# Two sections of small-tile work per chunk on TensorE, and new planning dates, in a fused linear recurrence and SwiGLU kernel

## The chip, the cores and the metric

The kernel runs on one core of a Trainium2 chip, in fp32. The metric is the time of one execution on the device in microseconds. TensorE multiplies matrices, VectorE (DVE) and ScalarE (ACT) work on elements, GpSimd (POOL) does a few small things, and SyncE (SP) issues most of the transfers. PSUM has eight banks, into which TensorE writes.

## The reference

```python
# attention block: batch 4, 8 heads, 768 steps, head size 48
scale = np.minimum(mag, 0.999) / (mag + 1e-06)          # mag = |a_re + i a_im|
a_re_n, a_im_n = (a_re * scale, a_im * scale)
for t in range(S):
    new_re = ar * S_re - ai * S_im                      # ar, ai: the gates of step t, per row d
    new_im = ar * S_im + ai * S_re
    kv = np.einsum('bhd,bhe->bhde', k[:, :, t], v[:, :, t])
    S_re, S_im = (new_re + kv, new_im)
    y[:, :, t] = np.einsum('bhd,bhde->bhe', q[:, :, t], S_re)
# then, on x = y as 3072 tokens of 384
rms = np.sqrt(np.mean(x * x, axis=-1, keepdims=True) + 1e-06)
xn = x / rms * rms_g
g = xn @ w_gate                                         # 384 x 1536
silu = g * (1.0 / (1.0 + np.exp(-g)))
val = xn @ w_val                                        # 384 x 1536
return (silu * val @ w_out).astype(np.float32)          # 1536 x 384
```

## The kernel before, in words

The sequence is cut into 24 chunks of 128 steps (six for each batch). The gates' cumulated products turn q and k into 96 rows per head (two parts of 48), so that a chunk's recurrence becomes matrix products. `attend(n)` does a chunk:

- **Scores.** k times q, four heads (one half) in a bank, in small tiles of 96 x 32. VectorE copies each half under a causal mask into `am` (COPY_PREDICATED).
- **y.** `am` times v (tiles `ve`), and q times the state of the chunk before, both in small tiles, into bank 6.
- **State.** k is transposed by TensorE with `ident` in full tiles, ScalarE copies the two halves into `kt`, and `kt` times v (tile `vn`) in small tiles makes the chunk's share of the state in bank 5. VectorE adds the old state and multiplies by the decay.
- **Norm.** ScalarE squares y into `sq`, VectorE adds its three parts, `ones` times `sq` on TensorE sums over the features into one column of bank 7. VectorE scales it into `ssv`, GpSimd raises it to the power -0.5 (`rs`), two transfers on the POOL queue spread it over the partitions (`sq<-rs`, `row<-sq`), and VectorE multiplies y by `row` into `xT`.

From the fifth chunk on (`n >= LATER`, 4) both halves of the scores use bank 5, one after the other, and both halves of the transposed k use bank 7. A work item of TensorE in small tiles carries `mode=BLK`; y and state are two items, which the planner may place apart.

Two chunks make a group of the feed-forward part. The first two groups use plain products (`feed`); the other ten use a bilinear scheme with fewer products (`joint`, with sums of `xT` in the tiles `yg` and `ve2`, of the weights in `in`, `rot`, `kq`, `am`), whose partial results go round the banks 0 to 4 by copies on ScalarE and sums on VectorE. The products with w_out (`wo`, `sums`, with `hT`) follow for each group.

Nothing is issued where it is written. Every operation is recorded by `add` with an estimated duration, what it reads and writes, and a date by which it is due; `schedule` then plays the engines forward in time and picks on each free engine the ready operation with the earliest date. That order is issued (all operations carry the line of `issue`, so tiles tell them apart). `shift` moves the dates of a stage of a chunk (such as ("norm", 16)) by so many microseconds. `between` adds a price where TensorE changes its tile, `grip` marks VectorE operations among SBUF tiles, `shy` GpSimd operations that are planned to wait for these.

The small tiles and full tiles meet in this planner like this:

```python
        if o["mode"] is not None:
            return 0.09
        return 0.13 if last["stage"][0] == "attend" else 0.01
```

Of the kernel before, what the change touches and what calls it, by code (L numbers as in the profile page):

```python
# [14 lines left out]
ALU = mybir.AluOpType  # L15
# [4 lines left out]
C = 128  # L20
BLK = 32
CAP = 0.999
EPS_MAG = 1e-6
EPS_RMS = 1e-6
# [476 lines left out]
class Flow:  # L501
# [9 lines left out]
    LANES = 8  # L511
    turn = 0.0
    patient = ("ACT", "DVE")
# [21 lines left out]

    def between(self, o, last):
# [41 lines left out]

    def add(self, eng, calls, dur, reads=(), writes=(), table=None, land=None, due=None, after=(), behind=(), late=None, mode=None, group=None):
# [4 lines left out]
        op = dict(i=len(self.ops), eng=eng, calls=calls, dur=dur, deps=set(), table=table, land=land, over=over, grip=grip, shy=shy,  # L584
                  base=due, late=late, mode=mode, group=group, stage=self.stage, behind={o["i"] for o in behind})
# [30 lines left out]
    def schedule(self):  # L616
        users = self.dates()
        left = [len(op["deps"]) + len(op["behind"]) for op in self.ops]
        ready = [0.0] * len(self.ops)
        free = {}  # L620
        waiting = {}
        table = None
        mode = last = None
        for op in self.ops:
            free.setdefault(op["eng"], self.BEGIN.get(op["eng"], 0.0))
            waiting.setdefault(op["eng"], [])
# [5 lines left out]
        served = held = 0.0  # L632
        order = 0

        def release(o, end, users=users):
            for u in users[o["i"]]:
                x = self.ops[u]
                ready[u] = max(ready[u], end + self.delay(o, x))
                left[u] -= 1
                if not left[u]:  # L640
                    waiting[x["eng"]].append(x)

        while True:
            best = None
            for eng, ops in waiting.items():
                if ops:
                    t = max(free[eng], min(ready[o["i"]] for o in ops))
                    if eng == "POOL":
                        t = min(max(free[eng], ready[o["i"]], held + 0.01 if o["shy"] else 0.0) for o in ops)
                    if eng == "SP" and len(sent) >= self.LANES:  # L650
# [18 lines left out]
            for o in waiting[eng]:  # L669
                if ready[o["i"]] > t + 1e-9 or o["shy"] and t < held:  # L670
                    continue
                key = o["due"]
                if o["table"] and table not in self.TABLES[o["table"]]:
                    key += self.switch
                if eng == "PE" and o["mode"] != mode:
                    key += self.turn
                if pick is None or key < pick[0]:
                    pick = (key, o)
            o = pick[1]
            if eng in self.patient:  # L680
                for x in waiting[eng]:
                    if t < ready[x["i"]] < t + o["dur"] - 0.2 and x["due"] < o["due"] - 50.0 and ready[x["i"]] < t + 1.5:
                        pick = None
                        free[eng] = max(free[eng], min(ready[y["i"]] for y in waiting[eng] if t < ready[y["i"]]))
                        break
                if pick is None:
                    continue
# [8 lines left out]
            if o["grip"]:  # L696
                held = t + dur
            if eng == "PE":
                dur += self.between(o, last)
                mode, last = o["mode"], o  # L700
# [6 lines left out]
            if eng == "PE":  # L707
                busy = sum(min(e, t) - max(b, t - 4.0) for b, e in recent if e > t - 4.0)
# [25 lines left out]
def fast(tc, ctx, qT, kT, v, a_re, a_im, w_gate, w_val, w_out, rms_g, out, H, bad):  # L734
# [48 lines left out]
    flow = Flow(nc, rooms)  # L783
    flow.switch = 4.0
    add = flow.add
# [94 lines left out]
    def mm_time(n, m=P):  # L880
        return 2 * max(0.844e-3 * n, 0.872e-3 * m)
# [346 lines left out]
    def attend(n):  # L1228
# [46 lines left out]
        order = [lines[c][i] for i in range(len(lines[0])) for c in range(4)]  # L1275
        mms(order, len(order) * mm_time(C) / 4 * 1.06, mode=BLK)
        flow.stage = "state", n
        if not last:
            kt = kts[0]
            for a in range(2):  # L1280
                ps = banks[7 - 3 * a] if n < LATER else banks[7]
                kp = ps[:, 0:HH * D2].rearrange("t (h d) -> t h d", h=HH)
                calls = [(nc.tensor.transpose, (kp[:, h], k[:, a * HH + h], ident[0:D2, 0:D2]), {})
                         for h in range(HH)]
                add("PE", calls, HH * 0.095, [k[:, a * HH:(a + 1) * HH], ident], [kp])
                act(kt[:, a * HH:(a + 1) * HH], kp, AF.Copy)
            ps = banks[5][0:D2, 0:DM]
            st = ps.rearrange("p (h d) -> p h d", h=H)
            mms([(st[c * BLK:(c + 1) * BLK, h], kt[:, h, c * BLK:(c + 1) * BLK], vv[:, h], True, True)
                 for h in range(H) for c in range(3)], H * 0.1, mode=BLK)  # L1290
            st4 = ps.rearrange("p (m e d) -> p m e d", m=NP, e=2)
# [338 lines left out]
    for in_, limit, op in ((ef, P_MIN, ALU.is_ge), (ef, 1.0, ALU.is_le), (range_, 0.0, ALU.is_le),  # L1630
# [17 lines left out]
    flow.shift = {  # L1648
        ("attend", 1): 2.0, ("attend", 2): -2.1, ("attend", 3): 16.0, ("attend", 4): 0.2, ("attend", 7): 4.7,
        ("attend", 14): -3.2, ("attend", 18): 6.6, ("decay", 1): 4.4, ("feed", 0): 15.4, ("feed", 1): 12.3,  # L1650
        ("feed", 2): 2.4, ("feed", 3): 0.1, ("feed", 4): 3.5, ("feed", 5): 22.0, ("feed", 6): 4.5,
        ("feed", 7): 47.1, ("feed", 8): -19.0, ("feed", 9): 11.6, ("feed", 10): 2.4, ("feed", 11): -11.1,
        ("form", 7): -0.2, ("form", 13): 6.0, ("load", 2): -16.5, ("load", 11): -2.1, ("look", 0): 9.4,
        ("look", 10): -10.6, ("norm", 16): -36.5, ("norm", 17): 36.0, ("norm", 22): -0.4, ("raw", 1): 19.8,
        ("root", 3): 2.8, ("root", 9): 0.2, ("root", 11): -9.6, ("rot", 3): -0.3, ("rot", 10): 58.8,
        ("scale", 0): 9.5, ("size", 0): 11.7, ("size", 3): 59.8, ("size", 8): -27.7, ("size", 10): 10.7,
        ("size", 11): -5.5, ("state", 0): 3.8, ("state", 3): -0.4, ("state", 4): -4.8, ("state", 6): -9.3,
        ("state", 7): -15.4, ("state", 10): -1.9, ("state", 13): -10.7, ("state", 16): 5.4, ("state", 18): 20.1,
        ("state", 21): -10.5, ("state", 22): 0.6, ("turn", 0): -1.4, ("turn", 1): 3.3, ("turn", 3): -0.4,
# [3 lines left out]
    }  # L1663
# [53 lines left out]
```

## Time and profile before

| | |
|---|---|
| three runs | 702.35, 703.12, 703.64 us; median 703.12 |
| span of the profiled execution | 699.7 us, from its first to its last instruction |
| TensorE busy | 648.4 us (93%) |
| weight loads of TensorE (beside its products) | 601.9 us (86%) |
| VectorE busy | 560.1 us (80%) |
| ScalarE busy | 506.9 us (72%), of that 67 table loads with 86.0 us |
| GpSimd busy | 71.5 us (10%) |
| mean granted TensorE clock | 0.995 |

A run's time is some 3 us above the span, since it holds what lies before the first and after the last instruction. In rows of the timeline stand the start in us from the beginning of the span, the duration, the engine, line and operation, the tile that is written and what it is made from, the TensorE tile (such as 96\*32), shapes and a count; in brackets the idle time before it and what ended it. An fp32 product shows as two MATMULs in the trace and as one row in an order of the program. A line of waits gives the total in us, how often, and the longest.

### The profile page before, as it was taken

To read this page: it belongs to the slowest core of one execution; us is meant where nothing else is said; L and a number is where in the kernel's file an instruction comes from. 1 tells how busy PE (TensorE), PEld (TensorE's weight loads), DVE (VectorE), ACT (ScalarE), POOL (GpSimd) and SP (SyncE) were. 2 spreads that over 40 slices of the span, in tenths; PEclk is the share of its full clock that TensorE was granted. 3 is DMA by queue.
4 is the path that set the end of the run, shared out by engine and by line. 5 is a ranking of instruction groups with operands and counts; after the bars stand their busy time and mean duration, and the time that the engine had idled before them with its cause. 6 is when DMAs were issued, how large, how long until landed. Compare 5 with 4: busy or idle time off the path is not lost.

```text
span 699.7 us, 18979 instructions
## 1 busy us (share of the span) xinstructions
PE 648.4 (93%) x7890; PEld 601.9 (86%) x7893; DVE 560.1 (80%) x1049; ACT 506.9 (72%) x850; POOL 71.5 (10%) x108
## 2 busy tenths in 40 slices
PE   0679999999997999999999999999999999899996
PEld 0569876886997989999999999989999989799996
DVE  7999999889987779879988969789789866255562
ACT  8677886993863974857787687685789676799860
POOL 3231030100013001001111001011000100000000
PEclk9999999999999999999999999999999999999999
DMA  9896575542334154254645205544422455744400
GB/s 293 266 282 152 148 229 147 128 81 73 90 56 81 35 116 75 70 119 87 160 89 104 69 5 115 141 84 75 118 70 55 110 118 142 244 138 155 139 1 29
DMA packets 104015, 82.02 MB, mean 117 GB/s; under 512 B 41936, under 2 KB 94416, under 8 KB 103920
## 3 DMA queue, kind: packets, MB, share of 16 engines
q1 hardware_dynamic: 98560, 64.78, 34.7%
q0 software_dynamic: 4416, 15.35, 10.2%
q8 instruction: 64, 1.05, 0.6%
q10 hardware_dynamic: 944, 0.59, 0.3%
q14 instruction: 31, 0.25, 0.1%
HBM read 55.84 MB, written 4.72 MB: 87 GB/s over the span
## 4 chain that ended last, share of the span: by engine, by line
PE 42%; issue 16%; DMA 14%; ACT 13%; DVE 10%; SPq 2%; POOL 2%; DVEq 0%; POOLq 0%; ACTq 0%
PE bank L731 42%; DMA wo<-in_w_gate_dram 3%; DMA in<-in_a_im_dram 2%; SPq L731 2%; ACT rot L731 2%; DVE hT L731 2%; ACT L731 2%; ACT hT L731 2%; ACT bank L731 1%; DMA sq<-rs 1%; DMA rot<-in_w_out_dram 1%; DVE wv L731 1%; ACT sg L731 1%; POOL rs L731 1%; ACT in L731 1%
## 5 line engine op out<-in xcount | busy, mean ns | idle before, releaser
L731 PE MATMUL bank<-wo,hT 128*128 128x192 f32 (+1 forms) x696 | 143.5, 352 | 1.1 <-DVE hT L731 0.9
L731 PEld LDWEIGHTS bank<-wo,hT 128*128 128x128 f32 x696 | 115.7, 191 | 12.8 <-DVE hT L731 1.8
L731 PE MATMUL bank<-xT,wg 128*128 128x128 f32 (+1 forms) x488 | 84.8, 306 | 5.6 <-DVE ot L731 3.7
L731 ACT ACT_TABLE_LOAD x67 | 86.0, 1283 | 3.4 <-issue 2.2
L731 PE MATMUL bank<-xT,wv 128*128 128x128 f32 (+1 forms) x488 | 82.6, 302 | 0.1
L731 ACT ACTIVATE hT<-bank 128x512 f32<-128x512 f32 x100 | 58.1, 594 | 31.4 <-PE bank L731 17.9
L731 PEld LDWEIGHTS bank<-xT,wg 128*128 128x128 f32 x488 | 70.4, 191 | 11.2 <-DVE ot L731 4.0
L731 POOL TENSOR_TENSOR rs<-ssv,mhalf 128x1 f32<-128x1 f32 x24 | 26.4, 1100 | 457.8 <-DVE ssv L731 457.8
L731 PEld LDWEIGHTS bank<-xT,wv 128*128 128x128 f32 x488 | 69.9, 191 | 3.5 <-DVE hT L731 0.5
L731 ACT ACTIVATE bank<-bank 128x512 f32<-128x512 f32 x60 | 35.1, 585 | 26.4 <-PE bank L731 19.9
L731 PE MATMUL bank<-yg,wg 128*128 128x128 f32 x320 | 50.7, 281 | 2.2 <-ACT hT L731 2.1
L731 DVE TENSOR_TENSOR hT<-hT 128x768 f32<-128x768 f32 (+1 forms) x60 | 51.7, 863 | 0.4
L731 PE MATMUL bank<-yg,wv 128*128 128x128 f32 x320 | 48.8, 275 | 0.0
L731 PEld LDWEIGHTS bank<-yg,wg 128*128 128x128 f32 x320 | 42.1, 191 | 4.1 <-ACT hT L731 3.0
L731 PE MATMUL bank<-sums,hT 128*128 128x192 f32 x240 | 45.1, 328 | 0.4 <-DVE hT L731 0.4
L731 ACT ACTIVATE sg<-bank 128x256 f32<-128x256 f32 (+1 forms) x72 | 38.5, 535 | 7.5 <-DVE ends L731 2.3
L731 PEld LDWEIGHTS bank<-yg,wv 128*128 128x128 f32 x320 | 42.2, 192 | 0.0
L731 DVE TENSOR_TENSOR hT<-bank,hT 128x512 f32<-128x512 f32 x50 | 34.3, 687 | 8.6 <-ACT bank L731 2.7
L731 DVE COPY_PREDICATED am<-causal,bank 128x512 f32<-128x512 int32 x48 | 34.9, 732 | 7.5 <-PE bank L731 7.3
L731 DVE TENSOR_TENSOR bank<-bank,hT 128x512 f32<-128x512 f32 x30 | 20.9, 697 | 24.9 <-ACT hT L731 16.4
L731 ACT ACTIVATE turns<-in 128x768 f32<-128x768 f32 (+1 forms) x39 | 30.7, 793 | 13.5 <-DVE in L731 7.4
L731 PEld LDWEIGHTS bank<-sums,hT 128*128 128x128 f32 x240 | 39.2, 190 | 0.7 <-DVE hT L731 0.5
(216 smaller groups left out, 1452.8 us busy)
## 6 DMA issues: line engine op xcount, KB each, us to landing
kq<-rot SPq DMA_DIRECT2D x84, 128.0 KB, 2.5
kq<-kin SPq DMA_DIRECT2D x60, 128.0 KB, 2.6
kin<-in_q_dram SPq DMA_DIRECT2D x24, 192.0 KB, 3.0
kin<-in_k_dram SPq DMA_DIRECT2D x24, 192.0 KB, 4.1
out_dram<-ot SPq DMA_DIRECT2D x23, 192.0 KB, 2.2
in<-in_a_re_dram SPq DMA_DIRECT2D x11, 384.0 KB, 4.8
in<-in_a_im_dram SPq DMA_DIRECT2D x11, 384.0 KB, 5.6
vn<-in_v_dram SPq DMA_DIRECT2D x20, 192.0 KB, 2.7
```

Source lines behind the costliest of these rows:

```text
L731: fn(*args, **kw)
```

## The change

1. From the fifth chunk on, the first half of the scores goes into bank 5 and the second into bank 7, and so do the two halves of the transposed k. Bank 7 is zeroed at the start like banks 4 and 5.
2. From the fifth chunk on, y and the state product are one work item of TensorE (except for the last chunk of a batch, which has no state product).
3. The planner's rules: entering small tiles costs 0.1 and leaving them 0.24 us (0.1 after an idle stretch); a product whose input comes late costs up to 0.1 us more; the landing of a transfer is planned with a margin of 0.3 to 2 us by stage; a change of tile counts 0.3 us when the next item is picked, a table load of ScalarE nothing (before 0 and 4). After the scaling of `ssv` no VectorE operation with `grip` is planned for 0.62 us (`hush`). All this holds from 120 us of planned time on.
4. The table `shift` is new: 242 entries in place of 70.

```diff
+    LEAVE, ENTER, LATE = 0.24, 0.1, 0.1
+    HUSH = 0.62
+    FROM = 120.0
+    MARGIN = {"load": 2.0, "kq": 2.0, "look": 2.0, "raw": 1.5, "attend": 1.5, "rot": 0.6, "decay": 0.6, "norm": 0.3}
+    turn = 0.3
+    switch = 0
...
+        if t < self.FROM:
+            return 0.09 if o["mode"] is not None else 0.13 if last["stage"][0] == "attend" else 0.01
         if o["mode"] is not None:
-            return 0.09
-        return 0.13 if last["stage"][0] == "attend" else 0.01
+            return self.ENTER
+        return self.LEAVE - 0.14 if idle > 0.14 else self.LEAVE
...
+        def able(o):
+            return max(ready[o["i"]], quiet) if o["grip"] else ready[o["i"]]
...
-                    key += self.switch
-                if eng == "PE" and o["mode"] != mode:
+                    key += self.switch if t > self.FROM else 4.0
+                if eng == "PE" and o["mode"] != mode and t > self.FROM:
                     key += self.turn
...
+            if o["hush"] and t > self.FROM:
+                quiet = t + dur + self.HUSH
...
+                if not more and t > self.FROM:
+                    late = ready[o["i"]] - (free["PE"] - self.LATE)
+                    if late > 0:
+                        dur += min(self.LATE, late)
...
-    for t in banks[4:6]:
+    for t in banks[4:6] + banks[7:]:
...
-            ps = banks[4 + a] if n < LATER else banks[5]
+            ps = banks[4 + a] if n < LATER else banks[5 + 2 * a]
...
-        mms(order, len(order) * mm_time(C) / 4 * 1.06, mode=BLK)
+        dur = len(order) * mm_time(C) / 4 * 1.06
+        if n < LATER or last:
+            mms(order, dur, mode=BLK)
...
-                ps = banks[7 - 3 * a] if n < LATER else banks[7]
+                ps = banks[7 - 3 * a] if n < LATER else banks[5 + 2 * a]
...
+            if n < LATER:
+                mms(todo, H * 0.1, mode=BLK)
+            else:
+                flow.stage = "y", n
+                mms(order + todo, dur + H * 0.1, mode=BLK)
...
-        ts(sv, col, 1.0 / DM, EPS_RMS, ALU.mult, ALU.add)
+        ts(sv, col, 1.0 / DM, EPS_RMS, ALU.mult, ALU.add, hush=True)
...
-        ("attend", 1): 2.0, ("attend", 2): -2.1, ("attend", 3): 16.0, ("attend", 4): 0.2, ("attend", 7): 4.7,
+        ("attend", 0): -2.8, ("attend", 1): -15.9, ("attend", 2): -25.3, ("attend", 3): -12.4, ("attend", 4): 37.8,
```

How the orders move, at three places. In TensorE's order the number after a name's underscore can be passed over: `bank5_70` is bank 5, `xT0_95` the tile xT0. First the scores of chunk 21, before: the end of the first half and the start of the second, both in bank 5.

```order
L731 MATMUL bank5_70<-kq0_107 32x32
L731 MATMUL bank3_68<-xT0_95,wg_91 128x128 x2
L731 MATMUL bank3_68<-xT0_95,wv_92 128x128 x2
L731 MATMUL bank4_69<-yg1_126,wg_91 128x128 x2
L731 MATMUL bank4_69<-yg1_126,wv_92 128x128 x2
L731 MATMUL bank5_70<-kq0_107 32x128
```

The same place now, in TensorE's order of the changed kernel: the halves' last and first rows.

```order
L751 MATMUL bank5_70<-kq0_107 32x96
L751 MATMUL bank5_70<-kq0_107 32x64
L751 MATMUL bank5_70<-kq0_107 32x32
L751 MATMUL bank7_72<-kq0_107 32x128
L751 MATMUL bank7_72<-kq0_107 32x96
L751 MATMUL bank7_72<-kq0_107 32x64
```

The four products between the halves are gone from there, and the second half is in bank 7. Over the chunks from the fifth on, the items in small tiles make 65 unbroken sections in TensorE's order before and 41 in the changed one.

Second, on TensorE, what follows the scores of the same chunk 21 in the changed kernel: the last row of the scores and the transposes of k (`ident_73,kq0`).

```order
L751 MATMUL bank7_72<-kq0_107 32x32
L751 MATMUL bank3_68<-wo_93,hT_94 128x192 x3
L751 MATMUL bank0_65<-xT0_95,wg_91 128x128 x2
L751 MATMUL bank0_65<-xT0_95,wv_92 128x128 x2
L751 MATMUL bank5_70<-ident_73,kq0_107 128x96 x4
L751 MATMUL bank1_66<-xT0_95,rot1_106 128x128 x2
L751 MATMUL bank1_66<-xT0_95,am1_116 128x128 x2
L751 MATMUL bank7_72<-ident_73,kq0_107 128x96 x4
```

Before, the transposes of this chunk wrote bank 7 ahead of its scores:

```order
L731 MATMUL bank7_72<-ident_73,kq0_107 128x96 x4
L731 MATMUL bank1_66<-ve2_120,rot1_106 128x128 x2
L731 MATMUL bank1_66<-ve2_120,kq1_108 128x128 x2
L731 MATMUL bank3_68<-yg1_126,in1_99 128x128 x2
L731 MATMUL bank3_68<-yg1_126,kq1_108 128x128 x2
L731 MATMUL bank4_69<-yg0_125,wg_91 128x128 x2
L731 MATMUL bank4_69<-yg0_125,wv_92 128x128 x2
L731 MATMUL bank5_70<-kq0_107 32x128
```

They now stand behind the scores, in the banks that VectorE's masked copies read.

Third, VectorE's order behind the mean square (`ssv`) of chunk 7, before:

```order
L731 TENSOR_SCALAR ssv_127<-bank7_72 128x1
L731 TENSOR_TENSOR hT_94<-bank1_66,mid0_136 128x256
L731 TENSOR_TENSOR hT_94<-hT_94 128x768
L731 TENSOR_TENSOR kin_100<-kin_100,turns_104 128x768
L731 TENSOR_TENSOR rot0_105<-kin_100,turns_104 128x768
L731 TENSOR_TENSOR t1_101<-t1_101,t2_102 128x768
```

The same place on VectorE in the changed kernel:

```order
L751 TENSOR_SCALAR ssv_127<-bank7_72 128x1
L751 TENSOR_TENSOR hT_94<-bank3_68,hT_94 128x512
L751 TENSOR_TENSOR hT_94<-hT_94 128x512
L751 TENSOR_TENSOR hT_94<-hT_94,mid1_137 128x256
L751 SCALAR_TENSOR_TENSOR t1_101<-t1_101,t4_103 128x768
L751 TENSOR_TENSOR hT_94<-hT_94,sg0_131 128x256
```

The operation right behind `ssv` reads a bank in both; now 512 columns wide in place of 256, and the long products among SBUF tiles (`kin`, `rot0`, `t1`) that came after have gone elsewhere.

More of the change, by code (lines that the diff above doesn't have):

```diff
@@ L511 @@
     LANES = 8
-    turn = 0.0
+    ENGINES = ("POOL", "ACT", "DVE", "SP", "PE")
+    LEAVE, ENTER, LATE = 0.24, 0.1, 0.1
[4 more added lines that the diff above has]
+    switch = 0
     patient = ("ACT", "DVE")
@@ L534, in delay, with between @@
         return 0.055 if x["eng"] == "PE" else 0.085 if x["eng"] == "POOL" else 0.034
-    def between(self, o, last):
+    def between(self, o, last, idle, t):
         if not last or o["mode"] == last["mode"]:
             return 0.0
+        if t < self.FROM:
+            return 0.09 if o["mode"] is not None else 0.13 if last["stage"][0] == "attend" else 0.01
         if o["mode"] is not None:
-            return 0.09
-        return 0.13 if last["stage"][0] == "attend" else 0.01
+            return self.ENTER
+        return self.LEAVE - 0.14 if idle > 0.14 else self.LEAVE
     def box(self, ap):
@@ L577, in note, with add @@
         self.seen[name] = kept
-    def add(self, eng, calls, dur, reads=(), writes=(), table=None, land=None, due=None, after=(), behind=(), late=None, mode=None, group=None):
+    def add(self, eng, calls, dur, reads=(), writes=(), table=None, land=None, due=None, after=(), behind=(), late=None, mode=None, group=None,
+            hush=False):
+        margin = self.MARGIN.get(self.stage[0], 0.0) if self.stage and self.stage[1] > 1 and land is not None else 0.0
         over = self.OVERLAP.get(eng, 0.0) if land is None else 0.0
@@ L584, in add @@
         op = dict(i=len(self.ops), eng=eng, calls=calls, dur=dur, deps=set(), table=table, land=land, over=over, grip=grip, shy=shy,
-                  base=due, late=late, mode=mode, group=group, stage=self.stage, behind={o["i"] for o in behind})
+                  base=due, late=late, mode=mode, group=group, stage=self.stage, margin=margin, hush=hush, behind={o["i"] for o in behind})
         self.ops.append(op)
@@ L619, in schedule @@
         ready = [0.0] * len(self.ops)
-        free = {}
-        waiting = {}
+        free = {eng: self.BEGIN.get(eng, 0.0) for eng in self.ENGINES}
+        waiting = {eng: [] for eng in self.ENGINES}
         table = None
@@ L631, in schedule @@
         recent = []
[L632 removed]
+        served = held = quiet = 0.0
         order = 0
@@ L637, in release @@
                 x = self.ops[u]
-                ready[u] = max(ready[u], end + self.delay(o, x))
+                margin = o["margin"] if users is not self.next and x["land"] is None and end > self.FROM else 0.0
+                ready[u] = max(ready[u], end + self.delay(o, x) + margin)
                 left[u] -= 1
@@ L641, in release @@
                     waiting[x["eng"]].append(x)
+        def able(o):
+            return max(ready[o["i"]], quiet) if o["grip"] else ready[o["i"]]
         while True:
             best = None
-            for eng, ops in waiting.items():
+            for eng in self.ENGINES:
+                ops = waiting[eng]
                 if ops:
-                    t = max(free[eng], min(ready[o["i"]] for o in ops))
                     if eng == "POOL":
                         t = min(max(free[eng], ready[o["i"]], held + 0.01 if o["shy"] else 0.0) for o in ops)
+                    else:
+                        t = max(free[eng], min(able(o) for o in ops))
                     if eng == "SP" and len(sent) >= self.LANES:
@@ L669, in schedule @@
             for o in waiting[eng]:
-                if ready[o["i"]] > t + 1e-9 or o["shy"] and t < held:
+                if able(o) > t + 1e-9 or o["shy"] and t < held:
                     continue
@@ L680, in schedule @@
             if eng in self.patient:
[L681 to L686, printed above, removed]
+                if any(t < able(x) < t + o["dur"] - 0.2 and x["due"] < o["due"] - 50.0 and able(x) < t + 1.5 for x in waiting[eng]):
+                    free[eng] = max(free[eng], min(able(x) for x in waiting[eng] if t < able(x)))
                     continue
@@ L697, in schedule @@
                 held = t + dur
+            if o["hush"] and t > self.FROM:
+                quiet = t + dur + self.HUSH
             if eng == "PE":
-                dur += self.between(o, last)
+                more = self.between(o, last, t - free["PE"], t)
+                dur += more
+                if not more and t > self.FROM:
+                    late = ready[o["i"]] - (free["PE"] - self.LATE)
+                    if late > 0:
+                        dur += min(self.LATE, late)
                 mode, last = o["mode"], o
@@ L707, in schedule @@
             if eng == "PE":
-                busy = sum(min(e, t) - max(b, t - 4.0) for b, e in recent if e > t - 4.0)
+                busy = 0.0
+                for b, e in recent:
+                    if e > t - 4.0:
+                        busy += min(e, t) - max(b, t - 4.0)
                 if busy < 2.0:
@@ L783, in fast @@
     flow = Flow(nc, rooms)
-    flow.switch = 4.0
     add = flow.add
@@ L1288, in attend @@
             st = ps.rearrange("p (h d) -> p h d", h=H)
-            mms([(st[c * BLK:(c + 1) * BLK, h], kt[:, h, c * BLK:(c + 1) * BLK], vv[:, h], True, True)
-                 for h in range(H) for c in range(3)], H * 0.1, mode=BLK)
+            todo = [(st[c * BLK:(c + 1) * BLK, h], kt[:, h, c * BLK:(c + 1) * BLK], vv[:, h], True, True)
+                    for h in range(H) for c in range(3)]
+            if n < LATER:
+                mms(todo, H * 0.1, mode=BLK)
+            else:
+                flow.stage = "y", n
+                mms(order + todo, dur + H * 0.1, mode=BLK)
+                flow.stage = "state", n
             st4 = ps.rearrange("p (m e d) -> p m e d", m=NP, e=2)
@@ L1654, in fast @@
[L1654 to L1658, printed above, removed]
@@ L1659, in fast @@
-        ("state", 21): -10.5, ("state", 22): 0.6, ("turn", 0): -1.4, ("turn", 1): 3.3, ("turn", 3): -0.4,
[3 rows of a table removed]
+        ("attend", 0): -2.8, ("attend", 1): -15.9, ("attend", 2): -25.3, ("attend", 3): -12.4, ("attend", 4): 37.8,
+        ("attend", 5): 16.9, ("attend", 6): -3.2, ("attend", 7): 1.8, ("attend", 8): 15.3, ("attend", 9): -124.5,
+        ("attend", 10): -36.0, ("attend", 11): 13.6, ("attend", 12): 58.3, ("attend", 13): -11.2, ("attend", 15): 0.3,
+        ("attend", 17): 22.3, ("attend", 18): -39.4, ("attend", 19): -6.6, ("attend", 20): -99.2,
@@ new lines, in fast @@
+        ("kq", 12): -23.2, ("load", 0): -39.9, ("load", 1): -10.1, ("load", 2): -586.6, ("load", 3): -7.4,
+        ("load", 4): -1.4, ("load", 5): 19.4, ("load", 6): -4.7, ("load", 7): -19.9, ("load", 8): -0.2,
+        ("load", 9): -133.6, ("load", 10): 75.9, ("load", 11): 0.3, ("load", 12): -78.0, ("look", 1): -1.6,
+        ("look", 2): -12.7, ("look", 3): -7.0, ("look", 4): 16.5, ("look", 5): 29.2, ("look", 6): 25.7,
+        ("look", 7): 48.2, ("look", 8): 19.0, ("look", 9): -65.3, ("look", 10): -16.7, ("look", 11): 0.4,
@@ new lines, in fast @@
+        ("look", 12): 64.5, ("look", 13): 26.5, ("look", 14): -0.1, ("look", 15): 6.6, ("look", 16): 18.5,
+        ("look", 17): -16.3, ("norm", 0): -144.1, ("norm", 1): 3.8, ("norm", 2): -13.4, ("norm", 3): 4.8,
+        ("norm", 4): 38.6, ("norm", 5): 35.3, ("norm", 6): 18.2, ("norm", 7): 0.3, ("norm", 8): 4.5,
+        ("norm", 9): -179.9, ("norm", 10): -41.4, ("norm", 11): 39.1, ("norm", 13): 11.7, ("norm", 14): -62.4,
+        ("norm", 15): -1.9, ("norm", 16): -532.3, ("norm", 17): -706.1, ("norm", 18): -19.3, ("norm", 19): -19.7,
@@ new lines, in fast @@
+        ("norm", 20): -31.6, ("norm", 21): 11.1, ("norm", 22): -45.0, ("norm", 23): -178.2, ("raw", 0): 2.6,
+        ("raw", 1): 44.6, ("raw", 2): 7.8, ("raw", 3): -16.3, ("raw", 4): 7.9, ("raw", 5): 0.3, ("raw", 6): -45.4,
+        ("raw", 7): 28.0, ("raw", 8): 51.3, ("raw", 9): 7.8, ("raw", 10): -36.8, ("raw", 11): 2.2,
+        ("root", 0): -109.6, ("root", 1): -69.0, ("root", 2): -6.0, ("root", 3): 5.3, ("root", 4): 202.0,
+        ("root", 5): 548.6, ("root", 6): 69.4, ("root", 7): -1.1, ("root", 8): 10.5, ("root", 9): -14.3,
@@ new lines, in fast @@
+        ("root", 10): 56.0, ("root", 12): 179.5, ("rot", 0): 49.1, ("rot", 1): 21.7, ("rot", 3): -5.4,
+        ("rot", 4): 85.2, ("rot", 5): 62.5, ("rot", 6): -444.0, ("rot", 7): 84.0, ("rot", 8): 707.5, ("rot", 9): 19.5,
+        ("rot", 10): 23.5, ("rot", 11): 0.1, ("rot", 12): -142.4, ("scale", 0): 799.1, ("size", 0): -37.1,
+        ("size", 1): -56.3, ("size", 2): -0.8, ("size", 3): 1260.4, ("size", 4): 81.1, ("size", 5): 62.5,
+        ("size", 6): 400.0, ("size", 7): 497.3, ("size", 8): 379.6, ("size", 9): 591.3, ("size", 10): -16.3,
@@ new lines, in fast @@
+        ("size", 11): 0.5, ("size", 12): -99.5, ("state", 0): 15.9, ("state", 1): 0.7, ("state", 2): 3.7,
+        ("state", 3): 5.9, ("state", 4): 1.8, ("state", 6): -265.5, ("state", 7): 4.3, ("state", 8): -11.5,
+        ("state", 9): -48.3, ("state", 10): 521.3, ("state", 12): 176.4, ("state", 13): -48.4, ("state", 14): 2.3,
+        ("state", 15): -47.5, ("state", 16): -15.4, ("state", 18): 4.3, ("state", 19): -124.4, ("state", 20): -79.4,
+        ("state", 21): -0.6, ("state", 22): 25.7, ("turn", 0): -153.9, ("turn", 1): 10.3, ("turn", 2): -1.6,
```

18 lines of the change are left out of this document (12 added, 6 removed), and 9 rows, old and new, of the table filler.

## The prediction, before the changed kernel ran

> **What bounds the kernel now.** I read the page first, then the engines' busy time by windows, TensorE's waits, and TensorE's timeline for what one change of tile costs.
>
> ```profile
> span 699.7 us, 18979 instructions
> PE 648.4 (93%) x7890; PEld 601.9 (86%) x7893; DVE 560.1 (80%) x1049; ACT 506.9 (72%) x850; POOL 71.5 (10%) x108
> PE   0679999999997999999999999999999999899996
> ```
> ```profile
> 110.00:690.00 580.00, 564.74 (x6822) 528.75 (x6823) 455.24 (x887) 421.75 (x725) 44.31 (x56) 1.00 0.40 97
> ```
> ```profile
> PE bank L731 <- ACT hT L731: 4.5, 5, 1.7
> PE bank L731 <- ACT bank L731: 4.0, 8, 2.3
> PE bank L731 <- DVE ot L731: 3.7, 1, 3.7
> PE bank L731 <- DMA kq<-kin: 1.4, 3, 0.5
> PE bank L731 <- DVE hT L731: 1.3, 4, 0.4
> ```
> The second fence is the window from 110 us, when the weights are in, to 690 us. TensorE (first figure after the length) is busy for 564.74 of 580 us; VectorE has 125 us free there and ScalarE 158. The third fence holds all of TensorE's named waits from 110 us on: 14.9 us, nearly the 15.3 us it is idle. So TensorE sets the time there: what is taken from its stream or its waits comes off the end. All twenty chunks that the change touches (from the fifth on) lie there; their first is at about 118 us.
>
> **The first term: the changes of tile.** These rows of TensorE's timeline (start, duration, group) show one half of a chunk's scores (32 of 96\*32) between 128\*128 products.
>
> ```profile
> 553.53 0.61 PE L731 MATMUL bank<-yg,wg 128*128 128x128 f32 x4
> 553.98 0.61 PE L731 MATMUL bank<-yg,wv 128*128 128x128 f32 x4
> 554.52 0.77 PE L731 MATMUL bank<-kq 96*32 96x128 f32 x32
> 555.22 0.71 PE L731 MATMUL bank<-xT,wg 128*128 128x128 f32 x4
> 555.77 0.61 PE L731 MATMUL bank<-xT,wv 128*128 128x128 f32 x4
> ```
> Durations overlap, so I go by starts. Four products take 0.45 us (553.53 to 553.98), but 0.54 when scores follow and 0.55 when scores came before (555.22 to 555.77): 0.09 to enter the small tile and 0.10 after leaving it. A third part hides inside a section:
>
> ```profile
> 33.71 1.33 PE L731 MATMUL bank<-kq 96*32 96x128 f32 x64
> 34.98 0.55 PE L731 MATMUL bank<-ident,kq 96*128 96x96 f32 x4
> ```
> ```profile
> 548.63 0.88 PE L731 MATMUL bank<-vn,kt 128*32 128x48 f32 x48
> 549.44 0.71 PE L731 MATMUL bank<-ve,wg 128*128 128x128 f32 x4
> ```
> ```profile
> 532.34 0.43 PE L731 MATMUL bank<-am,ve 128*32 128x128 f32 x8
> ...
> 534.23 2.06 PE L731 MATMUL bank<-wo,hT 128*128 128x192 f32 x11
> ```
> ```profile
> 559.88 0.84 PE L731 MATMUL bank<-vn,kt 128*32 128x48 f32 x45
> ...
> 562.46 0.71 PE L731 MATMUL bank<-xT,wg 128*128 128x128 f32 x4
> ```
> One half of the scores takes 0.70 us by itself (554.52 to 555.22), both halves in one section, as an early chunk has them, 1.27: 0.13 less than two. The state product takes 0.81 alone, y 1.89 alone, both joined 2.58: 0.12 less. So a section that is merged away saves 0.09 + 0.10 + 0.13 = 0.32 us, a fixed price that no engine covers. Counted in TensorE's order, the chunks from the fifth on make 65 sections in the kernel before (scores mostly 2, y and state 1 or 2 a chunk) and 41 in the changed one. 24 x 0.32 = **7.7 us off the path**. Its ends: 24 x 0.19 = 4.6 if the inner part is not won, 24 x 0.33 = 7.9 with the rows' rounding.
>
> **The second term: the order behind the mean square.** The longest wait has one visible cause.
>
> ```profile
> 209.28 0.14 DVE L731 TENSOR_SCALAR ssv<-bank 128x1 f32<-128x1 f32 x1
> 209.51 5.22 POOL L731 TENSOR_TENSOR rs<-ssv,mhalf 128x1 f32<-128x1 f32 x1 [13.23 <-DVE ssv L731]
> 209.68 0.94 DVE L731 TENSOR_TENSOR hT<-hT 128x768 f32<-128x768 f32 x1
> ...
> 214.14 0.56 DVE L731 TENSOR_SCALAR t<-t 128x768 f32<-128x768 f32 x1
> ...
> 215.03 0.59 POOL L731 DMA_DIRECT2D sq<-rs  x1 [0.29 <-POOL rs L731]
> ...
> 221.29 0.56 DVE L731 TENSOR_TENSOR xT<-bank,row 128x384 f32<-128x384 f32 x1 [3.83 <-DMA row<-sq]
> ...
> 224.44 0.71 PE L731 MATMUL bank<-xT,wg 128*128 128x128 f32 x4 [3.72 <-DVE ot L731]
> ```
> ```profile
> 220.00:230.00 10.00, 6.28 (x37) 5.98 (x36) 7.17 (x22) 3.03 (x5) 0.00 (x0) 0.83 0.20 61
> ```
> ```profile
> L731 POOL TENSOR_TENSOR rs<-ssv,mhalf x24: 558/772/5222, 40.8 to 646.3; 128x1 f32<-128x1 f32 x24
> ```
> GpSimd's power on one column, 0.56 us at best and 0.77 in the median (last fence: minimum, median, maximum in ns), ran 5.22 us and ended at 214.73, when VectorE's run of operations among SBUF tiles ended (214.14 + 0.56 = 214.70). Two transfers follow, then xT of the eighth chunk (7), then its group's sums, and TensorE stands for 3.7 us. The granted clock of that window is 0.83 in place of 1.00; 0.17 x 10 us is another 1.7 us. The change plans no such operation within 0.62 us of this column, and its order has a wider one that reads a bank there (512 columns in place of 256). The order also puts more work between this chunk's mean square and its group's first product: about 23 us of TensorE's stream in place of 8, an estimate from its rows at the durations above (a product of wo, 192 wide, counted 1.5 times). The chain took 15.2 us (209.28 to 224.44), of which some 4.5 was GpSimd's delay. I take the whole place as gained: **3.7 + 1.7 = 5.4 us**. Ends: 0, if another chain is as late there, and 5.4.
>
> **The rest, at nothing.** The new dates move nearly every operation after 70 us; up to there VectorE's and ScalarE's orders are the old ones but for one row, so the start is worth 0. The other 11.2 us of waits (14.9 - 3.7) are short; 2 us margins on planned transfers argue for fewer, the longer chain of a joined section for more. I leave them; ends -11.2 us (all gone) and the first rival's price. The state product now stands behind y in one section, so the norm's square and the release of kq start up to 0.81 us later and y waits for both copies of kt. Behind those wait the POOL queue's two transfers and the SP queue's three to six kq transfers of the next chunk. Cover: twenty chunks over the 580 us are 29 us each; without it, kq is late as in its row above, 1.4 / 3 = 0.5 us, at most 10 us over twenty chunks. One more bank is zeroed on VectorE before the first data are in: 0. ScalarE gets four more table loads:
>
> ```profile
> L731 ACT ACT_TABLE_LOAD x67 | 86.0, 1283 | 3.4 <-issue 2.2
> ```
> 4 x 1.28 = 5.1 us, hidden in its 158 us free; uncovered, +5.1 on the path.
>
> The Trainium skill (ScalarE: Activation LUTs, What ACT_TABLE_LOAD costs) counts against this: it gives 1283 ns and a drain of about 1380 ns, 2.66 us for each switch. By it the four would be an estimated 10.6 us of ScalarE, and the sum 700.5 if all of it fell on the path. This trace has the 1283 ns, but only 3.4 us idle before all 67 loads, so the drain hardly shows here.
>
> The sum: 699.7 - 7.7 - 5.4 = 686.6 us of span. The median of the three runs is 703.1, 3.4 us above the span shown, for what lies around it; I keep that: **690 us**.
>
> **The rivals.**
> *1, slower: the transposes wait for the masks.* They now go into the score banks 5 and 7, so they need VectorE's masked copies, which they didn't in bank 7 before. An early chunk with transposes right behind its scores shows the price:
>
> ```profile
> 36.29 0.55 PE L731 MATMUL bank<-ident,kq 96*128 96x96 f32 x4 [0.77 <-DVE am L731]
> ```
> ```profile
> 78.07 0.55 PE L731 MATMUL bank<-ident,kq 96*128 96x96 f32 x4 [0.68 <-DVE am L731]
> ```
> Twenty times 0.73 us is 14.6, above the 13.1 gained: 703.1 - 13.1 + 14.6 = 704.6 us. It decides from 0.66 us a chunk. Against it: the new order puts from 3 to 20 products (0.11 us times two each) between the scores and the first transposes nearly everywhere, and nothing stood between them in these rows.
> *2: the sections alone.* Another chain takes the place of the one at 224 us, or small waits add up to 5.4 us: 703.1 - 7.7 = 695.4. For it: 20 waits are left, and a faster TensorE comes sooner to each.
> *3: the waits go too.* With the margins half to all of the 11.2 us falls: 679 to 684 us.
> *4: no gain.* VectorE holds the stretches where it is full anyway, and the time given back there is found again as waits: 703. Against it: 455 of 580 us.
>
> **How the numbers follow.** My forecast, from 686 to 693 us: 0.37. Rival 2, 693 to 699: 0.25. Rival 3: 0.20. Rival 4: 0.07. Rival 1: 0.11. A measurement here can tell 0.2% (1.4 us) from no change. Faster takes the first three and a little of rival 4: 0.84; within 0.2%: 0.05; slower: 0.11. The range leaves out the lower part of rival 3 (0.08) and rival 1 (0.11): 681 to 701.
>
> **What would show it.** Right: 41 sections after 110 us, 1.27 us for the pairs of score halves, y with state at 2.58; no power on GpSimd above about 2 us after 170 us; no granted clock under 1 before 690. Wrong: TensorE waits for am or for ACT kt in a row of several us (rival 1), or the named waits still come to 15 us or more (rival 2). Far under 684 would mean that the dates did more than the sections.

## The result, and the profile after

The changed kernel takes 695.4 us (median of 4 runs, 694.99 to 695.89) where the kernel before took 702.7 (4 runs, 699.8 to 703.64): 0.9903 of the time, 95% interval 0.9882 to 0.9925, some 7 us faster. The forecast was 690 us with a range from 681 to 701; the time stands nearly on rival 2's number, 695.4.

The page of the changed kernel, with TensorE's busy tenths and the granted clock by slices of 17.3 us:

```profile
span 693.7 us, 19005 instructions
PE 647.2 (93%) x7893; PEld 606.5 (87%) x7893; DVE 561.8 (81%) x1050; ACT 511.2 (74%) x854; POOL 65.0 (9%) x108
PE   0599999999999999999999799999999998999996
PEclk9969999999999999999999899999999999999999
```
The span fell by 6.0 us. Past the start, one slice stands out, the 23rd: TensorE is 7 tenths busy there and the clock 8. Before, both rows were at 9 there. (The third slice's clock of 6 is taken up further down.)

TensorE's waits from 110 to 690 us (in all, times, longest), all but two of 0.2 us:

```profile
PE bank L751 <- DVE ot L751: 4.0, 1, 4.0
PE bank L751 <- ACT bank L751: 2.4, 7, 0.7
PE bank L751 <- DMA decay<-ends: 1.7, 1, 1.7
PE bank L751 <- DVE xT L751: 1.0, 1, 1.0
PE bank L751 <- DVE hT L751: 0.8, 3, 0.3
PE bank L751 <- DVE mid L751: 0.6, 1, 0.6
PE bank L751 <- ACT hT L751: 0.4, 1, 0.4
```
With those two they come to 11.3 us in place of 14.9. The row of 3.7 us for ot at 224 us is gone, and a row of 4.0 us for ot (the tile in which VectorE adds up a chunk's output) stands at the head: it is another wait, at 391 us.

The sections look as forecast. Both halves of a chunk's scores, and y with the state product (start, duration; the next start ends them):

```profile
546.19 1.33 PE L751 MATMUL bank<-kq 96*32 96x128 f32 x64
547.45 0.43 PE L751 MATMUL bank<-wo,hT 128*128 128x192 f32 x1
...
564.00 0.43 PE L751 MATMUL bank<-am,ve 128*32 128x128 f32 x8
...
565.78 0.86 PE L751 MATMUL bank<-vn,kt 128*32 128x48 f32 x48
566.57 0.71 PE L751 MATMUL bank<-ve,rot 128*128 128x128 f32 x4
```
1.26 us for the pair and 2.57 for y with state. The whole program has 51 sections for 75. At the prices that the starts of TensorE's rows give, times these counts, entering them costs 4.74 us for 6.97, the first product after them 4.63 for 6.62, the part inside 6.68 for 9.82. That is 7.4 us less. All other time beyond the products' own step, which is waits and stretches at half clock (a granted clock of 0.5), grew by 0.9 us: 4.8 less between 200 and 300 us, 5.2 less after 600, but 6.6 more between 300 and 400, and some 4 more in all elsewhere. The products themselves took 0.4 us longer.

What happens at 391 us, from the timeline of the changed kernel (chunk 14; VectorE and GpSimd, and TensorE from 391 us on):

```profile
377.88 0.15 DVE L751 TENSOR_SCALAR ssv<-bank 128x1 f32<-128x1 f32 x1
377.95 1.99 DVE L751 TENSOR_TENSOR_SCAN t<-t,t 128x128 f32<-128x128 f32 x6
378.12 3.10 POOL L751 TENSOR_TENSOR rs<-ssv,mhalf 128x1 f32<-128x1 f32 x1 [33.28 <-DVE ssv L751]
379.86 0.93 DVE L751 SCALAR_TENSOR_TENSOR in<-turns 128x768 f32<-128x768 f32 x1
380.93 0.35 DVE L751 TENSOR_TENSOR mid<-mid,bank 128x192 f32<-128x192 f32 x1
...
381.51 0.59 POOL L751 DMA_DIRECT2D sq<-rs  x1 [0.29 <-POOL rs L751]
...
387.35 0.54 POOL L751 DMA_DIRECT2D row<-sq  x1 [5.26 <-DMA sq<-rs]
391.41 0.56 DVE L751 TENSOR_TENSOR xT<-bank,row 128x384 f32<-128x384 f32 x1 [4.59 <-DMA row<-sq]
391.88 0.95 DVE L751 SCALAR_TENSOR_TENSOR t<-t,t 128x768 f32<-128x768 f32 x1
392.75 0.95 DVE L751 SCALAR_TENSOR_TENSOR in<-turns 128x768 f32<-128x768 int32 x1
393.62 0.95 DVE L751 SCALAR_TENSOR_TENSOR t<-t,t 128x768 f32<-128x768 f32 x1
394.49 0.55 DVE L751 TENSOR_TENSOR ot<-mid,bank 128x384 f32<-128x384 f32 x1
395.09 0.58 PE L751 MATMUL bank<-zeros 128*128 128x512 bf16 x1 [3.96 <-DVE ot L751]
395.60 2.36 PE L751 MATMUL bank<-kq 96*32 96x128 f32 x64
```
```profile
390.00:400.00 10.00, 6.04 (x86) 5.27 (x85) 6.08 (x10) 4.40 (x6) 0.00 (x0) 0.70 0.22 70
```
It reads like the place at 224 us before. GpSimd's power again ran long, 3.10 us. It ended at 381.21, 0.42 us after VectorE's first gap behind a row of operations on SBUF tiles (380.79 to 380.93). In the kernel before, VectorE's first gap stood at 214.10, 0.04 us long, and the power ended 0.63 us after it. The two transfers follow, xT of chunk 14 is late, and in VectorE's queue four operations stand behind it, the last of them ot, which frees the bank that TensorE's zeros matmul (it sets a bank to zero) wants. TensorE stands for 3.96 us. From 393.9 to 400.7 us its granted clock is 0.5, which makes 0.70 in the mean of this window (second fence): the score pair took 2.29 us in place of 1.26.

### The profile page after: what moved, and what is told of

Read it like the earlier page. It is cut to its first block, busy times and chain, and to the rows that moved or that the text cites. A ratio compares the mean times of both kernels' runs of the same rounds, so it can differ in the third digit from the quotient of the medians.

```text
span 693.7 us, 19005 instructions
## 1 busy us (share of the span) xinstructions
PE 647.2 (93%) x7893; PEld 606.5 (87%) x7893; DVE 561.8 (81%) x1050; ACT 511.2 (74%) x854; POOL 65.0 (9%) x108
## 4 chain that ended last, share of the span: by engine, by line
PE 50%; issue 17%; DVE 10%; ACT 10%; DMA 9%; POOL 1%; SPq 1%; ACTq 0%; POOLq 0%; DVEq 0%
PE bank L751 50%; DVE hT L751 3%; DMA sq<-rs 2%; ACT L751 2%; ACT t L751 1%; ACT hT L751 1%; DMA kq<-rot 1%; DVE turns L751 1%; SPq L751 1%; DMA in<-in_a_im_dram 1%; DMA row<-sq 1%; ACT in L751 1%; POOL rs L751 1%; ACT bank L751 1%; ACT turns L751 1%
## 5 line engine op out<-in xcount | busy, mean ns | idle before, releaser
L751 POOL TENSOR_TENSOR rs<-ssv,mhalf 128x1 f32<-128x1 f32 x24 | 19.0, 790 | 453.1 <-DVE ssv L751 424.8
L751 ACT ACTIVATE bank<-bank 128x512 f32<-128x512 f32 x60 | 34.9, 583 | 20.7 <-PE bank L751 16.5
L751 PEld LDWEIGHTS bank<-kq 96*32 96x32 f32 x1536 | 31.3, 114 | 11.9 <-issue 8.4
L751 DVE COPY_PREDICATED am<-causal,bank 128x512 f32<-128x512 int32 x48 | 32.9, 728 | 8.4 <-PE bank L751 8.1
L751 PE MATMUL bank<-am,ve 128*32 128x128 f32 x768 | 38.5, 286 | 1.0 <-DVE xT L751 1.0
```

Source lines behind the costliest of these rows:

```text
L751: fn(*args, **kw)
```

## The experiments

Ten of the twelve kernels keep the order of the kernel that they start from, but for the edit shown; two plan anew. Ratios are to the kernel before, run beside them on the same chip (its medians were 702.2 us beside struct_only, plan_only, split and before_line; 701.2 beside apart, joined, gap and xt_later; 701.3 beside the other four). The changed kernel's ratio is 0.9903; a hundredth is 7 us.

**One half of the change each, planned anew** (struct_only, plan_only).

```diff
 struct_only: the kernel before, and
+ps = banks[4 + a] if n < LATER else banks[5 + 2 * a]
+mms(order + todo, dur + H * 0.1, mode=BLK)      # y and state product
 plan_only: the changed kernel, and
-ps = banks[4 + a] if n < LATER else banks[5 + 2 * a]
+ps = banks[4 + a] if n < LATER else banks[5]
+mms(order, ...)   mms(todo, ...)                # y, and later the state product
```


> The kernel before with its own planner, rules and dates, and only the structural half of the change: score halves in banks 5 and 7, y and state product as one operation; its planner makes 58 sections in place of 75. Theory (sections alone): 17 x 0.33 = 5.6 us faster than before, about 697 us, and the wait at about 224 us with GpSimd's long power is still there, or its like elsewhere. Rival (the old order doesn't suit the longer section, so that masks, copies of kt or kq are late): TensorE's named waits after 110 us grow from 14.9 to 20 us or more and the time stays at 702 to 704 us or above.

> The changed kernel's planner rules and dates with the kernel before's structure: score halves in bank 5 one after the other, y and state product as two operations; 78 sections in place of before's 75. Theory (the gain is the sections; what the order gained at 224 us it gave back elsewhere): 702.7 + 3 x 0.33 = 703.7 us, within 2 us either way as its waits fall. Rival (the new rules and dates bring about 5 us by themselves): about 698 us.

Measured: struct_only 710.0 us, ratio 1.0104 (1.0057 to 1.0151); plan_only 743.8 us, ratio 1.0593 (1.0535 to 1.0650). Both are slower than the kernel before. The first rows of TensorE's waits after 110 us, of struct_only and then of plan_only:

```profile
PE bank L731 <- ACT bank L731: 5.8, 9, 1.4
PE bank L731 <- DVE xT L731: 5.3, 2, 4.2
```
```profile
PE bank L751 <- DVE xT L751: 8.0, 3, 7.1
PE bank L751 <- DMA kq<-kin: 6.6, 2, 6.2
```
All rows together come to 20.7 and 42.1 us. The starts of struct_only's rows give 5.2 us less for its 58 sections, near the 5.6 expected, and its rival came on top of it: waits and half clock grew by 17 us in the profiled execution, the slowest of its six (713.75 us). For plan_only neither expectation was near. The two are fresh plans, each with dates that were made for the other structure; so they don't say what a half is worth by itself.

**More sections, order frozen** (split).

```diff
+for n in range(LATER, N):   # second half of the scores behind the next product item
+    pe[x]["order"] = pe[x + 1]["order"] + 0.25
```


> The changed kernel with its order frozen, and one thing undone in it: in 17 chunks the second half of the scores runs one product item (a group's products into one bank) later than the first, so TensorE has 68 sections of small tiles in place of 51 over the whole program. Nothing else moves. Theory (a section has a fixed price on TensorE's own stream, about 0.33 us, that nothing covers): 17 x 0.33 = 5.6 us slower than the changed kernel, about 701.0 us. Rival (the time of the sections was given back as waits anyway, so that more sections only use up waits): 0 to 2 us slower, 695.4 to 697.4.

Measured: 715.0 us, ratio 1.0176 (1.0129 to 1.0224), 19 us above the changed kernel, over three times the theory. The sections' part is 5.0 us by the starts of the rows. The rest is waits and half clock: the named waits after 110 us come to 20.9 us for 11.3, among them one that the changed kernel doesn't have there:

```profile
PE bank L751 <- DVE am L751: 2.7, 7, 0.4
```
```profile
164.92 0.55 PE L751 MATMUL bank<-ident,kq 96*128 96x96 f32 x4
165.87 0.55 PE L751 MATMUL bank<-ident,kq 96*128 96x96 f32 x4 [0.39 <-DVE am L751]
```
These are the transposes of rival 1, waiting for the mask of the second half. So the edit is no clean test of the sections: a half that comes one product later also brings its mask later on VectorE, and everything behind that mask in VectorE's queue.

**More sections with nothing attached** (apart, joined).

```diff
+small = [(matmul, banks[6][c * BLK:(c + 1) * BLK, DM:DM + C], ident, ident) for c in range(4)]
 apart:  +flow.extra.append((order of a product ahead of y - 0.25, small))
 joined: +flow.extra.append((order of y - 0.25, small))
```


> The changed kernel, order frozen, plus 20 sections that do nothing useful: four small-tile matmuls on constants into columns of a bank that nobody reads, between two plain products, one ahead of the y of each chunk from the fifth on. Theory (a section has a fixed price on TensorE, 0.09 to enter, 0.06 to 0.10 after leaving, 0.13 inside, and 0.07 for the four matmuls themselves): 20 x 0.385 = 7.7 us slower than the changed kernel, 703.1 us. Rival (the stream has slack in front of its waits, which take most of it up): under 4 us slower, 699 us or less.

> The same 20 times four small-tile matmuls, but right ahead of the first matmul of the y section, so that no section is added (still 51). Theory (the price is for the section, not the matmuls): 20 x 0.07 = 1.4 us slower than the changed kernel, 696.8 us, so 6.3 us under the kernel with the same matmuls apart. Rival (the matmuls themselves, or their bank, cost it): as slow as the kernel with them apart, within 2 us.

Measured: apart 701.4 us, ratio 1.0005 (0.9979 to 1.0030), so 7.2 us above the changed kernel; joined 699.5 us, ratio 0.9982 (0.9959 to 1.0006), 5.5 above. One place of apart and one of joined:

```profile
402.90 0.43 PE L753 MATMUL bank<-ident 96*32 96x128 f32 x8
403.26 0.71 PE L753 MATMUL bank<-yg,wg 128*128 128x128 f32 x4
403.81 0.61 PE L753 MATMUL bank<-yg,wv 128*128 128x128 f32 x4
```
```profile
537.32 0.43 PE L753 MATMUL bank<-ident 96*32 96x128 f32 x8
537.56 0.40 PE L753 MATMUL bank<-am,ve 128*32 128x128 f32 x8
```
Inside a section that is there anyway the four matmuls took 0.225 us in the median, three times what I had put in: the 32 rows of a score half, 0.57 us, are 16 matmuls of two rows each, and 80 columns wide in the mean where these have 128. On their own they took 0.36, 0.13 more, and the product behind them 0.10 more. Over the 20 places the rows of apart give 6.3 us for sections and 4.5 for matmuls, 10.8 in all; those of joined 4.5. So the price of a section stands in the stream as forecast. At the end 7.2 of the 10.8 us arrived, and joined's 4.5 as 5.5. But the pair was the test of a section without its matmuls, and there the rival of joined came: the two kernels differ by 6.3 us in their streams and by only 1.6 at the end, some 2.4 us either way. The waits say where some of it went (ot's row in apart, then in joined):

```profile
PE bank L753 <- DVE ot L753: 2.1, 1, 2.1
```
```profile
PE bank L753 <- DVE ot L753: 4.0, 2, 3.1
```
The wait at 391 us fell from 4.0 to 2.1 and 3.1 us: what TensorE does ahead of it is partly paid out of it.

**The long power** (before_line, before_gap, gap, after_line). The line replaces the power in all chunks, so the power itself isn't computed; the gap puts two reads of a bank on VectorE behind one column.

```diff
 line: -gpsimd.tensor_tensor(rs, ssv, mhalf, pow)
       +vector.tensor_scalar(rs, ssv, -0.5, 1.5, mult, add)   # right behind ssv
 gap:  +2 * vector.tensor_scalar(scratch, col.to_broadcast([P, 192]), 1.0, 0.0, mult, add)
       # behind ssv of chunk 7 (before_gap) or of chunk 14 (gap)
```


> The kernel before with its order frozen, and the power -0.5 of the mean square's column replaced by a straight line (-0.5 x + 1.5) on VectorE right behind the column: GpSimd's operation and its two hand-overs are left out in all chunks (the power itself isn't computed). Theory (GpSimd's power ran 5.22 us because VectorE's operations among SBUF tiles held it off, and that made TensorE wait 3.7 us at 224 us and run at a clock of 0.83 there): 4.0 to 5.4 us faster than before, 697.3 to 698.7 us, no wait for ot of 3.7 us at 224 us. Rival (VectorE's queue or the two transfers make that chain late anyway): under 1.5 us faster, 701 to 703 us.

> The kernel before, order frozen, with the same two VectorE reads of a bank (192 elements each into a scratch tile) behind the mean square's column of chunk 7 alone. Theory (that one power of 5.22 us is what the place at 224 us cost): the power takes under 1 us there, TensorE's 3.7 us and the half clock go, 4.0 to 5.4 us faster than before, as the straight line in all chunks was (5.5). Rival (the straight line won its time by the other chunks' powers or hand-overs): under 2 us.

> The changed kernel, order frozen, and two operations added on VectorE right behind the mean square's column of chunk 14: the column, read from its bank, spread over 192 elements of a scratch tile that nobody reads, 0.2 to 0.3 us each, so that VectorE reads a bank, not SBUF tiles alone, while GpSimd starts its power. Theory (the six scans behind it held GpSimd off, 3.10 us in place of 0.56): the power takes under 1 us, the row lands about 2.5 us earlier and TensorE's wait at 391 us falls from 3.96 to about 1.5: 2 to 3.5 us faster than the changed kernel, 691.9 to 693.4 us. Rival (GpSimd is held off all the same, or the two transfers take as long until their next free slot): within 1 us of 695.4.

> The changed kernel, order frozen, with the power replaced by the straight line (-0.5 x + 1.5) on VectorE in all chunks, as it was done to the kernel before (the power itself isn't computed). Theory (only the power of chunk 14 is on the path): as fast as with the two reads at chunk 14, 0.983 to 0.985 of the time before, and so 6 to 7.5 us under the kernel before with the straight line, which is the sections' 7.4 us. Rival (other long powers, 2.2 us at 88 us and 1.97 at 174, cost too): 0.982 or less.

Measured: before_line 696.7 us, ratio 0.9929 (0.9903 to 0.9955); before_gap 696.3 us, 0.9928 (0.9898 to 0.9958); gap 689.2 us, 0.9837 (0.9807 to 0.9866); after_line 692.4 us, 0.9864 (0.9817 to 0.9910). GpSimd's rows in before_gap and in gap:

```profile
209.66 0.56 POOL L731 TENSOR_TENSOR rs<-ssv,mhalf 128x1 f32<-128x1 f32 x1 [13.23 <-DVE ssv L731]
210.52 0.59 POOL L731 DMA_DIRECT2D sq<-rs  x1 [0.29 <-POOL rs L731]
213.03 0.54 POOL L731 DMA_DIRECT2D row<-sq  x1 [1.93 <-DMA sq<-rs]
```
```profile
378.25 0.73 DVE L751 TENSOR_SCALAR scratch<-bank 128x192 f32<-128x192 f32 x2
378.42 0.56 POOL L751 TENSOR_TENSOR rs<-ssv,mhalf 128x1 f32<-128x1 f32 x1 [33.34 <-DVE ssv L751]
...
387.29 0.56 DVE L751 TENSOR_TENSOR xT<-bank,row 128x384 f32<-128x384 f32 x1 [0.17 <-DMA row<-sq]
```
Two reads of a bank, 0.65 us of VectorE, brought one power from 5.22 to 0.56 us and another from 3.10 to 0.56. At both places TensorE's wait is gone. That shows the cause at both, and their worth: 5.0 us at 224 us in the kernel before (702.2 and 701.3 times 0.0071 to 0.0072), 4.6 us at 391 us in the changed one (0.9903 to 0.9837). The Trainium skill (SBUF — State Buffer, Who interferes with whom) states that a VectorE instruction with two SBUF inputs contends with a GpSimd instruction that reads SBUF; the scans behind the column have two, the added reads of a bank have none. Both cures agree with it; three scans shown at the end do not. In gap the gain was more than the 2 to 3.5 us of its theory, which had left the two transfers as they were; they are taken up at the end too. The straight line in the changed kernel gained 2.7 us, less than the two reads and short of its theory, within intervals that overlap. Its profiled execution lost 5 us more to waits and half clock between 60 and 110 us than that of gap (the clock was 0.5 for 6.8 us from 86.5 on), and its six times spread from 689.5 to 697.6 us where gap's lie between 688.6 and 690.3. Why is open. No price of the other long powers (such as 1.97 us at 174 us) shows in it, but a small one could hide in that spread.

**The queue's order** (xt_later, both).

```diff
+spread[14]["order"] = to["order"] + 0.25        # xT of chunk 14 behind the next ot on VectorE
 both: with the gap at chunk 14 too
```


> The changed kernel, order frozen, and one operation moved: on VectorE the xT of chunk 14, which waits for its row from a transfer until 391.4 us, goes behind the ot that TensorE's zeros matmul waits for at 391 us. Theory (head of the line: the operations behind xT in VectorE's queue were ready, so TensorE's 3.96 us are lost to the queue's order): the wait goes and the granted clock stays at 1.00 there, 4.0 to 5.3 us faster than the changed kernel, 690.1 to 691.4 us. Rival (ot or the work behind it is late for another reason): under 1 us, 694.4 us or more.

> The changed kernel, order frozen, with both cures for the wait at 391 us: the two reads at chunk 14, and its xT behind ot. Theory (they remove the same wait): within 1 us of the better of the two, 0.982 to 0.984 of the time before. Rival (each removes a wait of its own): 0.977 or less.

Measured: xt_later 687.9 us, ratio 0.9829 (0.9793 to 0.9866); both 690.3 us, 0.9833 (0.9797 to 0.9869). VectorE in xt_later, then GpSimd's powers there (minimum, median, maximum):

```profile
388.58 0.55 DVE L751 TENSOR_TENSOR ot<-mid,bank 128x384 f32<-128x384 f32 x1
389.56 0.56 DVE L751 TENSOR_TENSOR xT<-bank,row 128x384 f32<-128x384 f32 x1 [0.42 <-DMA row<-sq]
```
```profile
L751 POOL TENSOR_TENSOR rs<-ssv,mhalf x24: 547/564/3099, 41.4 to 624.5; 128x1 f32<-128x1 f32 x24
```
```profile
390.00:400.00 10.00, 10.00 (x231) 9.44 (x231) 8.68 (x15) 8.81 (x17) 0.00 (x0) 1.00 0.38 106
```
The power is as long as ever, and the wait is gone with it late: ot ran at 388.58, xT when its row was there, TensorE was busy throughout at full clock. 5.2 us against the changed kernel, by moving one operation over four others. So the wait needs both: a late row, and xT ahead of ot in the queue. Both cures together gain no more than one, as the theory said. Each of these three versions beats both kernels, by 4.6 to 5.2 us on the changed one; among themselves they can't be told apart.

**Sections where that wait is gone** (gap_apart).

> The changed kernel with the two reads at chunk 14 and the 20 useless sections between products together. In the stream a useless section took 0.54 us (0.316 for the section, 0.225 for its four matmuls), 20 of them 10.8 us; without the two reads they made the kernel only 7.2 us slower. Theory (the wait at 391 us took part of them up, and where it is gone they cost what they take): 10 to 11 us above the kernel with the reads alone, about 1.000 of the time before. Rival (other small waits take up as much, or the rows' price isn't the price at the end): 6 to 8 us above, about 0.994.

Measured: 697.4 us, ratio 0.9938 (0.9915 to 0.9962), 7.1 us above gap: the rival's figure. My theory that the wait at 391 us had taken up the rest falls. In the profiled executions the stream grew by 10.8 us, and the waits and half clock after 110 us fell by 3.6, in many places: no single wait of TensorE is above 1.1 us there. (Ahead of 110 us they grew by some 3.) So small waits seem to pay for a part of what is put in front of them. How large a part is not settled: the interval of the difference is about 2.7 us either way.

## Why the prediction was right or wrong

**The bound** was right. What came off or went onto TensorE's stream or its waits moved the time, though not one for one.

**First term, the changes of tile: 7.7 us; the rows show 7.4.** The count (41 sections from the fifth chunk on), 1.26 and 2.57 us for the joined sections, and the price of 0.09 + 0.10 + 0.13 us stand as written; split and apart repeat it. "A fixed price that no engine covers" was too strong: of 10.8 us put into the stream some 7 arrived, twice, and of the 6.3 us between apart and joined 1.6. With the long power cured on both sides, the changed kernel is at 0.9837 and the kernel before at 0.9928: 6.4 us, with some 3 us either way. That fits the 7.4 us of the rows, but the two orders differ in more than sections, so what the sections alone are worth at the end is not shown.

**Second term, the order behind the mean square: 5.4 us forecast, about nothing net.** The step that failed is "I take the whole place as gained". The cause was right (before_gap) and so was its size, 5.0 us at the end. The place at 224 us did go. But the same chain came up at 391 us and cost 4.6 us. I had argued that the change plans no such operation within 0.62 us of the column. Six scans stand 0.07 us behind the column of chunk 14, each with two tiles of SBUF, and the planner's rule doesn't count scans. The rule told what the planner avoids, not what stands there; the rows of the changed order on VectorE behind each of the 20 columns would have shown it. Two of my own lines for "right" are what the profile broke: no power above about 2 us after 170 us (3.10 us at 378), and no granted clock under 1 before 690 (0.70 from 390 to 400).

**The rest at nothing.** The other named waits after 110 us fell from 11.2 to 7.3 us; with half clock, and with what lies ahead of 110 us, the whole program outside the stretch from 200 to 400 us lost 0.9 us less than before. That is the sum of gains and losses that no experiment tells apart, the largest a gain of 5.2 us after 600 us. The four table loads cost nothing that shows (with 10.6 us for them the sum would have been 700.6, not 700.5). The start didn't stay as it was: the third slice of the granted clock reads 6, where the kernel before had 9 in every slice, and 2.5 us more went in waits and half clock before 60 us. It doesn't seem to reach the end: the changed kernel's runs with a mean clock of 0.983 took 695.43 and 694.99 us, those with 0.989 and 0.991 took 695.33 and 695.89. Nor is it fixed by the order: gap has the same order there, and its third slice reads 9.

**Around the span.** I kept 3.4 us from the median's distance; the runs after show 1.7 us between a run's span and its time (693.7 and 695.43, 700.4 and 702.16). So the execution shown of the kernel before was one of about 701.4 us by this estimate, and 1.7 us of my 3.4 was the spread of its runs, which reach from 697 to 707 us.

**The rivals.** Rival 2 came, by the mechanism it names and at its number: another chain took the place of the one at 224 us. That the time is 695.4 to the tenth is luck, since gains and losses of several us elsewhere happen to cancel. It had 0.25, the forecast 0.37; with the rows behind the columns read, they would have changed places. Its other sign, named waits of 15 us or more, did not come (11.3): it is one place, not many. Rival 1 did not come, and split shows that it was real: with the second half one product later in 17 chunks, seven waits for am came, 2.7 us in all. Rivals 3 and 4 are out: 679 to 684 and 703 us.

## What to carry to other kernels

Price a merged section from the stream, but expect less of it at the end, and test how much; and before counting a cured stall as gained, look for the same pattern everywhere in the new order, row by row, since a planner's rule covers only the operations that it counts. When an engine is found waiting on another engine's in-order queue, look at what stands at the head of that queue: moving one operation that isn't urgent was worth as much here as curing the delay itself, 5.2 us beside the 7 or so of the whole change. Dates fitted to one structure needn't suit another: each half of this change, planned with dates that were not made for it, was slower than none, so parts are better tested in a frozen order.

## What the runs showed of the hardware that was not expected

The long power is no matter of luck: behind the same six scans it took 3.095 to 3.099 us in all five kernels that had them (the changed one, split, apart, joined, xt_later). Yet behind three scans it took 0.60, though it began 0.167 us after the first scan in both places:

```profile
276.73 1.04 DVE L751 TENSOR_TENSOR_SCAN t<-t,t 128x128 f32<-128x128 f32 x3
276.89 0.60 POOL L751 TENSOR_TENSOR rs<-ssv,mhalf 128x1 f32<-128x1 f32 x1 [14.83 <-DVE ssv L751]
```
Why three let it through and six do not is open. The transfer behind the late power was slower too. GpSimd's queue in gap:

```profile
379.27 0.59 POOL L751 DMA_DIRECT2D sq<-rs  x1 [0.29 <-POOL rs L751]
382.05 0.53 POOL L751 DMA_DIRECT2D row<-sq  x1 [2.19 <-DMA sq<-rs]
```
From the first issue to the second are 2.78 us here, and 5.84 in the changed kernel (381.51 to 387.35), where the transfer began 2.2 us later. The second transfer went the other way: from its issue to xT are 5.24 us here and 4.06 in the changed kernel. So a cure of 2.5 us on the power brought the row 4.1 us earlier (xT at 387.29 for 391.41), though the chain began 0.3 us later. What the first transfer met in the 3 us was not tried.
